# Linear attention and a Fourier gate on one core: a new order of work on all five engines, the negated filter spectrum read from PSUM, zero matmuls between PE's work

## The chip, the core and the metric

The kernel runs on one core of a Trainium2 chip. Inputs lie in the chip's memory as float32 and the output goes back there as float32. The metric is the time of one execution in device microseconds (us), as the median of several runs; lower is better. TensorE (PE) multiplies matrices into PSUM, VectorE (DVE), ScalarE (ACT) and GpSimd (POOL) work elementwise, and SyncE (SP) issues most transfers. Each engine works through its own list in order and waits where an operand is not there yet.

## The reference

```python
# r, k, v, w: (batch 4, heads 8, seq 768, head_dim 48); u: (8, 48)
for t in range(S):
    cur = np.einsum('bhd,bhe->bhde', u[None] * kt, vt)
    y[:, :, t] = np.einsum('bhd,bhde->bhe', rt, state + cur)
    state = wt[:, :, :, None] * state + np.einsum('bhd,bhe->bhde', kt, vt)
# x: y as (4, 768, 384)
proj = x @ w_proj                      # 384 x 1152
x1, x2, x3 = proj split in three
X2 = np.fft.rfft(x2, n=S, axis=1)
H = np.fft.rfft(filter_fft, n=S, axis=0)[None, :, :]
out = (x1 * np.fft.irfft(X2 * H, n=S, axis=1) * x3) @ w_out
```

The first half is a recurrence with a decay `w` and a bonus `u`, for 32 pairs of batch and head. The second half is a gate: three projections, a circular convolution by Fourier transforms over the sequence, two products and an output projection.

## The kernel before

The sequence is cut into 24 chunks of 128 steps, 6 to a batch. Chunks are loaded in groups: 0 and 1 alone, then pairs. A load (`lw`, `lk`, `lr`, `lv`) brings one chunk of w, k, r or v, 192 KB in pieces of 192 bytes, through SP's queue. Three buffers hold w and four each hold k with r, and v.

A group takes the logarithm of w (`ln`, ACT, L1250), a bf16 copy of v (`vb`), the product r k (`rk`), times u (`ru`), halves it by an add (`rh`), sums it over a head (`cc`, DVE, L1263) and multiplies v by the sums (`vc`, the bonus term, L1158). Any of `rk`, `ru`, `rh` stands on POOL or DVE, as the order says.

A chunk then goes through these steps: sums of the logarithms by triangular matmuls (`cs`, PE, L1278 to L1281), their exponential in PSUM (`ex`, ACT, L1284), the products with k and r (`kq`, DVE, L1287), the decay of the chunk (`ph`, ACT), eight transposes (`tr`, PE, L1299) and their copy (`qk`, DVE or ACT), the scores (`sc`, PE, L1311), the causal mask (`mt`, with `D` or `M` a product with a mask on DVE, L1327, with `A` or `N` a copy on ACT that POOL cuts afterwards, `mc`, L1332; `M`, `N` and `C` take both halves at once), the state (`ki`, `kv` on PE, `su` on DVE, L1362), the output of the chunk in PSUM (`yi` puts in the bonus term by two matmuls, `ys` the state's part, `y` the scores' part), its copy to `xn`, three transposes (`yt`) and their copy into `xT` (L1164 or L1162). Where `yi` is `-`, `xn` has the letter `V` and adds the bonus term on DVE (L1401).

Once a batch is whole, `second(b)` runs: the projections `p` and `q` (L1536) and `xw` (L1573), their copies `cp`, `cxw` and the product `cq`, folded sums and differences `sd`, the forward transform `f` with its copy `cf`, the products with the filter's spectrum `u0`, `u1`, `p`, the inverse transform `E` with its copy `cE` and two adds `aE`, the gate product `yE`, and the output `o` with its copy `co` and its store `so`. Batches overlap: one batch's second half runs between the chunks of the next. Projection weights come through POOL's queue (`wproj0` to `wproj2`, L1227, float32 to bf16 on the way).

The filter's spectrum is made once (`spectrum`, L1493): `filt` is one load of 1152 KB through SP's queue, `fsd0` and `fsd1` fold it on DVE (L1498), `h0` to `h2` transform it on PE into two PSUM banks each, `hc` scales it on ACT into `hh[:, 0]` (L1504), and `hg` on DVE copies the real part (L1510) and writes the negated imaginary part (L1514) into `hh[:, 1]`, from `hh[:, 0]`, which lies in SBUF. The tables of the inverse transform get their mirrored parts by four sign multiplications (`if`, L1482 to L1486).

What runs where and when is one list, `ORDER`, written out in the source: a line has a step's name, its engine's letter, the PSUM bank where it needs one, and in some lines another step's name. `Plan.run` (L1040) emits the steps in that order. The last name, where there is one, ties a step to an earlier DVE step: it waits until that one is done. `warm n b` emits `n` matmuls of zeros, 256 wide, into bank `b` (L1191). The list in before starts with 30 of them. Further on the list runs as

```
lk7 S
lk6 S
lr6 S
...
filt S
```

and has `if` on POOL between `mc9.0` and `rk6`, `wproj1` behind `mc3.1` and `wproj0` behind `mc4.0`.

Of the kernel before, what the change touches and what calls it, by code (L numbers as in the profile page):

```python
# [181 lines left out]
mc3.1 G
wproj1 G
ex4 A
cc2 D
kq4 D
ph4 A
su3 D
yt1 P 1
xT1 D  # L190
vc2 G su2
mc3.0 -
xT0 D
ex5 A
kq5 D
ph5 A
tr4 P 0
yi3 P 2
yi2 P 4
ys3 P  # L200
ys2 P
y3 P
y2 P
lr6 S
qk4 D
lr7 S
# [31 lines left out]
cxw0.0 D
lv7 S
mc4.0 G mt5.0  # L240
yi4 P 3
ys5 P
ys4 P
y4 P
mc5.0 -
xn4 A
y5 P
xn5 D
cs6 P 0
lv6 S  # L250
lw9 S
yt4 P 2
# [11 lines left out]
cxw0.4 A
lk8 S
lr9 S
lv8 S
tr6 P 5
# [11 lines left out]
wproj0 G  # L280
lv9 S
lw10 S
p0.2.1 P 4
p0.2.0 P 5
cf0.0 A
mt6.0 N
p0.0.1 P 0
rk4 D
sd0.1.0 D
cp0.2.0 D  # L290
f0.2 P 5
p0.0.0 P 2
# [1 line left out]
cp0.0.0 A
sc7 P 6
lr10 S
lr11 S
lw11 S
ru4 D
cp0.0.1 D  # L300
fsd0 D
mc6.0 C
ln5 A
lk11 S
fsd1 D
h1 P 0
mt7.0 M
h2 P 2
lv10 S
mc6.1 -  # L310
# [12 lines left out]
lv13 S
kv6 P 3
hg2 D
su6 D
mc7.1 -
yi6 - 2
hc0 A
hg0 D  # L330
cs8 P 0
yi7 P 4
# [1 line left out]
y6 P
ys7 P
ex8 A
y7 P
xn6 V
cs9 P 6
xn7 A  # L340
ki7 P 2
kv7 P
kq8 D
yt7 P 3
yt6 P 5
tr8 P 4
su7 D
lr12 S
lv11 S
# [52 lines left out]
ln6 A
q0.0.0 P 4
u00.0 D
cq0.0.1 D
q0.2.0 P 7
ki9 P 6
# [50 lines left out]
mc10.1 -
y10 P
xn10 A  # L460
mt11.1 -
kq12 D
su10 D
cs13 P 6
lk14 S
lk15 S
ex13 A
lw14 S
mc11.1 -
lr15 S  # L470
lw15 S
lk16 S
lv14 S
E0.0 P 3
# [152 lines left out]
mc14.1 -
y14 P
ln10 A
ex17 A  # L630
kq17 D
xw2.0 P 4
# [1 line left out]
mc15.0 -
xn14 A
mt16.0 A
ph17 A
yi15 P 2
ys15 P
y15 P  # L640
cxw2.0 A
xn15 A
cs18 P 6
# [45 lines left out]
ys16 P
q2.0.0 P 4  # L690
mc16.0 G
cq2.2.0 D
mt17.0 N
su18 D
y16 P
mt17.1 -
ln11 A
mc17.1 -
lv23 S
o0.0 P 2  # L700
rk11 G cc10
mc17.0 C
ru11 G
vc10 G rh10
xn16 V
sc18 P 0
lv22 S
cs20 P 6
co0.0 A
mt18.1 -  # L710
cq2.0.0 D
ex20 A
mt18.0 M
tr19 P 5
o0.1 P 2
# [1075 lines left out]
```

## Time and profile before

| what | value |
|---|---|
| runs | 166.23, 167.73 and 168.83 us; median 167.73 |
| profiled execution | 167.69 us, of it 165.9 in the span from the first to the last instruction |
| mean granted PE clock | 0.931 of full speed |
| busy, share of the span | PE 144.2 us (87%), DVE 140.3 (85%), ACT 117.7 (71%), POOL 99.3 (60%) |
| chain that ended last | PE 29%, DVE 22%, POOL 15%, DMA 12%, issue 11%, ACT 7% |
| memory | 22.41 MB read and 4.72 MB written, 164 GB/s over the span |

The page divides the span into 40 equal slices; a digit is the busy share in tenths. "Idle before" is the time an engine stood still just ahead of an instruction, with the one whose end released it behind an arrow. A matmul's own duration has its way through the array in it; what one costs in a row is the distance between starts. A line number such as L1158 can be that of a helper with many uses, so the tile's name beside it says which step it is.

### The profile page before, as it was taken

The page shows a single profiled execution, that of the slowest core. Times are in us where ns is not written, and L with a number is a line of the kernel's source. Part 1 is how long each engine was busy: PE and PEld are TensorE (multiplying, and loading weights), DVE is VectorE, ACT ScalarE, POOL GpSimd, SP SyncE. Part 2 cuts the span into 40 slices and gives each one's busy share as a digit, 9 for nine tenths or more (in the row PEclk, how much of TensorE's full clock was granted, in tenths as well). Part 3 has the DMA queues.
Part 4 walks back from the last instruction along what each step waited for, and adds up shares of the span by engine and source line. Part 5 has one row for each costly group of instructions (what it writes and reads, how often), then busy time and mean ns, then how long its engine had stood idle before and what let it go on. Part 6 is the DMA issues. An engine that isn't in the chain of part 4 may idle for free.

```text
span 165.9 us, 4290 instructions
## 1 busy us (share of the span) xinstructions
PE 144.2 (87%) x1665; PEld 94.9 (57%) x1665; DVE 140.3 (85%) x259; ACT 117.7 (71%) x192; POOL 99.3 (60%) x103
## 2 busy tenths in 40 slices
PE   7868877984984999649999999999989999999980
PEld 5538655652543667344666677667567666655530
DVE  6758999892799889375899999999999999999950
ACT  4997956674274686634998988878989866785460
POOL 7967796602227059985695799699269680330320
PEclk9965999998699599965999999999999999999997
DMA  5999999899999989999999999900250000200936
GB/s 107 212 212 215 207 199 203 161 287 194 211 212 175 203 166 205 184 217 214 201 192 217 191 211 184 175 11 0 96 194 0 4 0 4 95 2 19 356 133 254
DMA packets 104118, 26.23 MB, mean 158 GB/s; under 512 B 100129, under 2 KB 102690, under 8 KB 104098
## 3 DMA queue, kind: packets, MB, share of 16 engines
q1 hardware_dynamic: 102498, 24.78, 68.1%
q0 software_dynamic: 1600, 1.18, 5.0%
...
HBM read 22.41 MB, written 4.72 MB: 164 GB/s over the span
## 4 chain that ended last, share of the span: by engine, by line
PE 29%; DVE 22%; POOL 15%; DMA 12%; issue 11%; ACT 7%; SPq 1%; POOLq 0%; ACTq 0%; DVEq 0%
PE banks L1536 6%; POOL rk L1158 6%; DMA wproj<-in_moe_w_proj_dram 5%; PE banks L1438 5%; PE banks L1299 4%; DMA out_dram<-o 3%; PE banks L1692 3%; PE banks L1573 3%; POOL mt L1332 3%; DVE kq L1287 3%; PE banks L1628 2%; DVE hh L1514 2%; DMA w<-in_w_dram 2%; DMA kr<-in_k_dram 2%; POOL vc L1158 2%
## 5 line engine op out<-in xcount | busy, mean ns | idle before, releaser
L1536 PE MATMUL banks<-xT,wproj 128*128 128x384 bf16 x144 | 29.8, 344 | 2.7 <-DMA wproj<-in_moe_w_proj_dram 2.1
L1332 POOL TENSOR_SCALAR_AFFINE_SELECT mt<-mt 128x512 bf16<-128x512 bf16 (+1 forms) x17 | 15.9, 937 | 16.5 <-ACT mt L1162 11.8
L1158 POOL TENSOR_TENSOR vc<-vb,cc 128x768 bf16<-128x768 bf16 (+1 forms) x13 | 18.3, 1410 | 10.6 <-DVE cc L1263 7.6
L1287 DVE TENSOR_TENSOR kq<-banks,kr 128x768 bf16<-128x768 f32 x24 | 22.7, 950 | 2.2 <-ACT banks L1284 1.9
L1162 ACT ACTIVATE x<-banks 128x768 bf16<-128x768 f32 (+1 forms) x26 | 18.0, 700 | 6.1 <-PE banks L1573 4.0
L1158 POOL TENSOR_TENSOR rk<-kr 128x768 bf16<-128x768 f32 (+1 forms) x12 | 20.1, 1679 | 2.6 <-DMA kr<-in_r_dram 1.3
L1299 PE MATMUL banks<-ident,kq 128*128 128x128 bf16 x192 | 16.8, 243 | 5.1 <-DVE kq L1287 4.5
L1536 PEld LDWEIGHTS <-wproj 128*128 128x128 bf16 x144 | 13.5, 102 | 11.9 <-DMA wproj<-in_moe_w_proj_dram 2.5
L1284 ACT ACTIVATE banks<-banks 128x768 f32<-128x768 f32 x24 | 19.1, 804 | 0.5 <-PE banks L1281 0.2
L1299 PEld LDWEIGHTS <-kq 128*128 128x128 bf16 x192 | 13.6, 110 | 7.3 <-DVE kq L1287 6.7
L1327 DVE TENSOR_TENSOR mt<-banks,mask_excl 128x512 bf16<-128x512 f32 (+1 forms) x17 | 15.6, 934 | 2.4 <-PE banks L1311 2.0
L1162 ACT ACTIVATE qk<-banks 128x1024 bf16<-128x1024 bf16 x14 | 14.1, 1028 | 2.4 <-PE banks L1299 2.3
L1162 ACT ACTIVATE X<-banks 128x768 bf16<-128x768 f32 x12 | 9.7, 811 | 7.8 <-PE banks L1438 7.5
L1162 ACT ACTIVATE mt<-banks 128x512 bf16<-128x512 f32 (+1 forms) x17 | 12.6, 749 | 3.7 <-PE banks L1311 3.1
L1158 POOL TENSOR_TENSOR y<-y,g 128x768 bf16<-128x768 bf16 (+1 forms) x6 | 8.1, 1354 | 11.6 <-PE banks L1628 9.0
L1438 PE MATMUL banks<-sd,F 128*128 128x384 bf16 (+1 forms) x96 | 14.0, 336 | 0.3 <-DVE sd L1584 0.3
L1573 PE MATMUL banks<-wproj,xT 128*128 128x384 bf16 x72 | 14.0, 333 | 0.1
L1692 PE MATMUL banks<-wout,y 128*128 128x384 bf16 x72 | 13.2, 326 | 0.0
L1438 PEld LDWEIGHTS <-F 128*128 128x128 bf16 (+1 forms) x120 | 9.1, 106 | 7.0 <-issue 2.9
L1561 DVE TENSOR_TENSOR g<-banks,x 128x384 bf16<-128x384 f32 (+1 forms) x16 | 11.6, 747 | 0.2 <-PE banks L1536 0.2
L1162 ACT ACTIVATE o<-banks 128x768 f32<-128x768 f32 (+1 forms) x12 | 9.1, 782 | 3.6 <-PE banks L1692 1.9
L1158 DVE TENSOR_TENSOR U<-X,hh 128x2304 bf16<-128x2304 bf16 (+1 forms) x12 | 11.1, 950 | 0.0
(110 smaller groups left out, 331.0 us busy)
## 6 DMA issues: line engine op xcount, KB each, us to landing
w<-in_w_dram SPq DMA_DIRECT2D x24, 192.0 KB, 3.9
kr<-in_r_dram SPq DMA_DIRECT2D x24, 192.0 KB, 3.8
kr<-in_k_dram SPq DMA_DIRECT2D x24, 192.0 KB, 3.8
v<-in_v_dram SPq DMA_DIRECT2D x24, 192.0 KB, 4.2
...
U<-in_moe_filter_fft_dram SPq DMA_DIRECT2D x1, 1152.0 KB, 9.3
wproj<-in_moe_w_proj_dram POOLq DMA_DIRECT2D x3, 288.0 KB, 5.8
out_dram<-o SPq DMA_DIRECT2D x2, 192.0 KB, 2.6
```

Of the source, the lines that this page charges most:

```text
L1158: return eng(e).tensor_mul(o, a, b)
L1162: return nc.scalar.activation(out=o, in_=a, func=AF.Copy)
L1284: op(f"ex{i}", [ACT], lambda e, bk: nc.scalar.activation(out=two(bk, f"cs{i}")[:, :, 0:C], in_=two(bk, f"cs{i}")[:, :, 0:C], func=AF.Exp), ...
L1287: op(f"kq{i}", [DVE], lambda e, bk: nc.vector.tensor_mul(kq[f][:, :, :, 0:D], two(bk, f"cs{i}")[:, :, 0:C].rearrange("p a (h d) -> p a h d ...
L1299: nc.tensor.transpose(p[:, HP * m + j, :], kq[f][:, m, 2 * j:2 * j + 2, :], ident)
L1327: return copy(ACT, o, x) if e in (ACT, ACT2) else nc.vector.tensor_mul(o, x, _mid(mask_excl, z - HP * a))
L1332: return nc.gpsimd.affine_select(out=o, in_=o, pattern=[[0, z - HP * a], [1, L]], compare_op=ALU.is_gt, fill=0.0, base=0, channel_multipli ...
L1438: nc.tensor.matmul(p[rows], F[:, ti, c0 + rows.start:c0 + rows.stop], x[q][:, ti, :], start=(ti == 0), stop=(ti == NT - 1),)
L1536: nc.tensor.matmul(p, wproj[:, cb, col0:col0 + L], xT[bx][:, cb, sl], start=(cb == 0), stop=(cb == CB - 1),)
L1561: op("c" + n3, [DVE], lambda e, bk: nc.vector.tensor_mul(g[bx][:, fs, sl], view(bk, n3), x1[:, fs, sl]), r=[f"x1.{fb}.{hf}" for fb in fbs] ...
L1573: nc.tensor.matmul(view(bk)[:, z], xT[bx][:, cb, (c0 + z) * L:(c0 + z + 1) * L], wproj[:, cb, C:2 * C], start=(cb == 0), stop=(cb == CB - 1),)
L1692: nc.tensor.matmul(view(bk)[:, z], yt_[:, z, :], wout[:, cb, :], start=(cb == 0), stop=(cb == CB - 1),)
```

## The change

It has four parts, and touches nothing of what is computed.

1. `hg` reads the imaginary part from PSUM, where `h` left it, and scales it by -2/S in the same instruction (for the first block by a column `neg0`, whose first row is 0). The first row of the copied block is still set by a copy and a memset. `hg` now counts as a user of the PSUM banks of `h`.
2. `warm` stands at nine places: 28 at the start, 11 behind `um`, then 2, 5, 3, 3, 7, 2 and 6, between the first chunks and the filter's transform. In all 67 in place of 30.
3. `xn` has a new letter `X`: ACT copies to a float32 buffer `xf`, and a new POOL step `xa` adds the bonus term and writes `xn`. One chunk, 18, uses it; for the others `xa` is `-`.
4. The whole list stands in another order, with other engines for some 80 steps and other banks and ties. Among them: `if` goes from POOL to DVE, ahead of chunk 6; `wproj1` and `wproj0` stand one behind the other; `p0.2.0`, `p0.0.0`, `p0.2.1` and `xw0.4` stand ahead of `cs6`; `rk4` goes to POOL; six `qk` go from DVE to ACT and one the other way; seven `xT` go from DVE to ACT and three back; `yi6` and `yi13` are added, `yi10`, `yi14` and `yi18` dropped; nine `mc` are added on POOL and nine dropped; `yE0.1`, `yE0.2`, `yE1.1` and `yE3.2.0` go from POOL to DVE and `yE1.0` the other way. Loads start `lk1 lw2 lr0 lk0` in place of `lw0 lr0 lk0 lk1`; `lw22` and `lw23` go out near the end.

```diff
-ADD, DVE2, ACT2, POOL2, FOLD = "V", "M", "N", "C", "Q"
+ADD, DVE2, ACT2, POOL2, FOLD, WIDE = "V", "M", "N", "C", "Q", "X"
...
-warm 30 7
+warm 28 7
...
+um P 1
+warm 11 7
...
+wproj1 G su1
+wproj0 G mt3.0
...
+kq5 D
...
+if D
+xT2 D
+vb3 G kq4
...
+warm 7 6
+sc6 P 4
...
+sc7 P 2
...
+warm 6 6
+h1 P 6
+mt7.1 D
+mt7.0 D
+mc6.1 -
+h2 P 0
...
-if G
-rk6 G rh5
...
+xn18 X
+q2.0.1 P 0
...
+xa18 G kq22
...
+    xf = sb.tile([L, NX, C], FP32, name="xf")
...
+    neg0 = sb.tile([L, 1], FP32, name="neg0")
...
+        nc.vector.memset(neg0, -2.0 / S)
+        nc.vector.memset(neg0[0:1, :], 0.0)
...
-            o = xn[:, i % NX].rearrange("p (j a d) -> p a j d", a=2, d=D)
+            o = (xf if e == WIDE else xn)[:, i % NX].rearrange("p (j a d) -> p a j d", a=2, d=D)
...
-            return copy(e, o, yview(bk))
...
+            return copy(ACT if e == WIDE else e, o, yview(bk))
...
+        op(f"xa{i}", [POOL, NONE], lambda e, bk: nc.gpsimd.tensor_add(
+            xn[:, i % NX], xf[:, i % NX], vcq.rearrange("p h d -> p (h d)")),
+           r=[f"xn.{i % NX}", f"vc.{fg}"], w=[f"xn.{i % NX}"])
...
                 nc.vector.tensor_scalar(
-                    out=hh[:, 1, 0, n, :], in0=hh[:, 0, 1, n, :], scalar1=-1.0, scalar2=None, op0=ALU.mult)
+                    out=hh[:, 1, 0, n, :], in0=two(bk, f"h{n}")[:, 1, 0:C], scalar1=-2.0 / S if n else neg0,
+                    scalar2=None, op0=ALU.mult)
...
-            op(f"hg{n}", [DVE], gcopy(n), r=[f"Hc.{n}"], w=[f"H.{n}"])
+            op(f"hg{n}", [DVE], gcopy(n), r=[f"Hc.{n}"], w=[f"H.{n}"], uses=[f"h{n}"])
```

More of the change, by code (lines that the diff above doesn't have):

```diff
@@ L180 @@
-ki3 P 4
-kv3 P
[L182 to L187, printed above, removed]
-su3 D
[L189 to L206, printed above, removed]
+lr6 S
+xT0 D
+yi3 P 6
+ys3 P
+y3 P
+ex5 A
+yi2 P 2
+ys2 P
+filt S
+kq4 D
+xn3 A
+mc2.0 -
+y2 P
+xn2 A
+lw9 S
+ph4 A
+wproj1 G su1
+wproj0 G mt3.0
+lv6 S
+xa3 -
+rk3 G xT0
+xa1 -
+tr4 P 6
+yt1 P 0
+kq5 D
+ki3 P 3
+xa2 -
+yt3 P 2
+lw8 S
+qk4 A
+ph5 A
+xT1 A
+lv7 S
+lr9 S
+lk9 S
+yt2 P 7
+kv3 P
@@ L235 @@
-yi5 P 5
 mc5.1 -
-ln4 A
[L238 to L252, printed above, removed]
+ys4 P
+y5 P
+y4 P
+p0.2.0 P 1
+xn5 D
+xa5 -
+yt5 P 2
+cxw0.0 A
+xn4 A
+xa4 -
+ln4 A
+yt4 P 5
 xT4 D
-yt5 P 5
+p0.0.0 P 6
 xT5 D
-cs7 P 3
+cp0.2.0 D
+lv8 S
+p0.2.1 P 4
+xw0.4 P 2
+cp0.0.0 A
+cs6 P 6
+cp0.2.1 A
+cs7 P 4
+p0.0.1 P 0
+cxw0.4 A
+sd0.0.0 D
+f0.0 P 2
 ex6 A
-lw8 S
 ex7 A
 kq6 D
-xw0.4 P 6
 kq7 D
 ph6 A
[L264 to L268, printed above, removed]
@@ L269 @@
-qk6 D
-tr7 P 0
-ph7 A
-lr8 S
-qk7 A
-lk9 S
-sd0.0.0 D
-sc6 P 2
+ph7 A
+rk4 G
+tr6 P 7
+lw10 S
+lw11 S
+sd0.1.0 D
+cp0.0.1 A
+tr7 P 4
+qk7 A
+f0.2 P 0
+qk6 A
+cf0.0 A
+warm 7 6
+sc6 P 4
+ru4 D
 mt6.1 -
-f0.0 P 6
+fsd0 D
+fsd1 D
+warm 2 6
+sc7 P 2
 lk10 S
[L280 to L292, printed above, removed]
-cf0.2 A
[L294 to L310, printed above, removed]
+lk11 S
+cf0.2 A
 rh4 D
 cc4 D
-mt7.1 -
+vb4 G
+mt6.0 N
+warm 6 6
[4 more added lines that the diff above has]
+h2 P 0
+mc7.0 -
+ln5 A
+vc4 G cc4
+mc7.1 -
 hc1 A
 hg1 D
-mc7.0 -
-h0 P 6
+h0 P 4
+mc6.0 C cc4
+kv6 P 3
 hc2 A
-cp0.2.1 A
-vb4 G xT4
-vc4 G fsd0
-lw13 S
[L323 to L332, printed above, removed]
-wproj2 G
[L334 to L349, printed above, removed]
@@ L350 @@
-ex9 A
-lr14 S
-xT6 D
+hg2 D
+lr11 S
+cs8 P 6
+hc0 A
+lk15 S
+ex8 A
+su6 D
+yi7 P 0
+ys7 P
+y7 P
+hg0 D
+xn7 A
+xa7 -
+lv11 S
+lw12 S
+lv10 S
+lk12 S
+lw13 S
+yi6 P 2
+y6 P
+cs9 P 4
+xn6 A
+yt7 P 1
+ex9 A
+xa6 -
+ki7 P 0
+kq8 D
+yt6 P 3
+xT7 D
+lr12 S
+kv7 P
+ph8 A
+wproj2 G
+xT6 D
+lk13 S
+tr8 P 1
+rk5 G hg0
+qk8 A
+xw1.0 P 6
 kq9 D
-lw12 S
-rk5 G
 ru5 D
@@ L397 @@
+mt9.1 A
+mc9.1 G
+mc9.0 G su7
+yi8 P 2
+q0.2.1 P 7
+u10.0 D
+cq0.0.1 D
+ln6 A
+lk14 S
+lr14 S
+ys9 P
+ys8 P
+y8 P
+cq0.2.1 D
+q0.0.0 P 0
+u00.0 D
 xn8 A
-yt8 P 6
-u10.0 D
-cq0.2.1 D
+xa8 -
+yt8 P 3
 xT8 A
[L402 to L407, printed above, removed]
-y9 P
+y9 P
+cs11 P 6
+xn9 A
+q0.2.0 P 2
 cq0.0.0 D
-xn9 A
-cs11 P 0
+ex11 A
+ki9 P 3
 kv9 P
-ex11 A
-yt9 P 3
+xa9 -
+yt9 P 0
+xT9 A
 cs10 P 4
 cq0.2.0 D
-xT9 A
+p1.2.0 P 2
+rk6 G cq0.2.1
 ex10 A
+kq11 D
+ph11 A
+ru6 D
 su9 D
-kq11 D
@@ L458 @@
[L458 to L461, printed above, removed]
-kq12 D
[L463 to L474, printed above, removed]
+lw16 S
+q1.0.0 P 0
+qk11 D
+sc10 P 4
+lr17 S
+vb6 G kq10
+vc6 G kq10
+mt10.1 A
+mc10.1 G cc6
+cq1.0.0 D
+sc11 P 6
+mt11.1 A
+mc11.1 G
+mt10.0 D
+yi10 - 4
+q1.2.0 P 3
+ki10 P 2
+lr16 S
+lk16 S
+lv16 S
+cs12 P 0
+mt11.0 A
+cq1.2.0 D
+mc11.0 G qk11
+mc10.0 -
+ys10 P
+y10 P
+xn10 V
+cs13 P 6
+rk7 G
+ru7 G
+rh7 G
+kv10 P
+ex12 A
+ex13 A
+kq12 D
+xa10 -
 yt10 P 5
-tr12 P 2
@@ L627 @@
[L627 to L632, printed above, removed]
-mt16.1 D
[L634 to L643, printed above, removed]
+xn13 A
+xa13 -
+cs17 P 0
+tr16 P 6
+ex17 A
+lw21 S
+yt13 P 4
+xT13 A
+yt12 P 5
+qk16 D
+ys14 P
+xT12 A
+y14 P
+ki16 P 7
+kv16 P
+mc15.1 -
+lk21 S
+lr20 S
+lk20 S
+ln10 A
+sc16 P 4
+mt16.0 A
+xn14 V
+kq17 D
+lv21 S
+xa14 -
+yt14 P 6
+lk22 S
+lv20 S
+xw2.0 P 2
+mc15.0 -
+ph17 A
+lr23 S
+yi15 P 0
+ys15 P
+rk9 G mt15.0
+xT14 A
+ru9 D
+rh9 G qk16
+cxw2.0 A
@@ L686 @@
-yi16 - 6
-sc17 P 2
-cc10 D
[L689 to L715, printed above, removed]
+cc9 D
+q2.2.0 P 2
+cs19 P 4
+qk17 A
+ex19 A
+p2.0.0 P 0
+lw23 S
+ph18 A
+vc9 G
+tr18 P 3
+kq19 D
+cp2.0.0 A
+xw2.2 P 6
+vb10 A
+qk18 D
+p2.2.0 P 1
+ph19 A
+sc17 P 4
+cxw2.2 A
+kv18 P 3
+q2.0.0 P 6
+yE0.2 D
+mc16.0 G
```

1072 lines of the change are left out of this document (525 added, 547 removed).

## The prediction

> **What bounds the kernel now.** I read the page's slices first, then a table of four stretches, then the timeline of each engine at the stretches' borders. The borders are the first k-by-decay products (`kq`, L1287) of chunks 6, 8 and 12, since nothing of a chunk runs on VectorE before its own.
>
> ```profile
> span 165.9 us, 4290 instructions
> PE   7868877984984999649999999999989999999980
> DVE  6758999892799889375899999999999999999950
> PEclk9965999998699599965999999999999999999997
> DMA  5999999899999989999999999900250000200936
> 33.30:54.60 21.30, 15.49 (x138) 8.76 (x137) 16.98 (x24) 11.02 (x17) 6.25 (x5) 0.91 1.06 215
> 54.60:80.20 25.60, 21.86 (x247) 14.46 (x246) 17.91 (x26) 16.27 (x28) 17.20 (x14) 0.81 1.01 199
> 80.20:159.20 79.00, 78.17 (x924) 51.36 (x922) 78.18 (x139) 63.30 (x107) 49.83 (x40) 1.00 0.47 110
> ```
>
> The columns of the last three rows are length, then busy time of PE, PEld, DVE, ACT and POOL, the granted clock, DMA share and GB/s. From 80.2 us on DVE and PE are both busy 78.2 of 79 us: that stretch costs what its work costs. Before it DVE stands 4.3 us idle in the second stretch and 7.7 us in the third, and the clock falls. The loads keep the DMA full to about 107 us, so nothing can come before its data. Time is to be had in the two middle stretches.
>
> ```profile
> 33.29 1.88 DVE L1287 TENSOR_TENSOR kq<-banks,kr 128x768 bf16<-128x768 f32 x2
> 43.91 2.62 DVE L1498 TENSOR_TENSOR P<-U 128x1152 bf16<-128x1152 f32 x2
> 48.77 1.53 DVE L1514 TENSOR_SCALAR hh<-hh 128x384 bf16<-128x384 bf16 x1
> 50.39 2.51 DVE L1514 TENSOR_SCALAR hh<-hh 128x384 bf16<-128x384 bf16 x1
> 53.96 0.26 DVE L1514 TENSOR_SCALAR hh<-hh 128x384 bf16<-128x384 bf16 x1
> 54.60 0.95 DVE L1287 TENSOR_TENSOR kq<-banks,kr 128x768 bf16<-128x768 f32 x1
> 48.66 1.52 POOL L1158 TENSOR_TENSOR vc<-vb,cc 128x768 bf16<-128x768 bf16 x1 [5.91 <-DVE cc L1263]
> 50.96 1.81 POOL L1158 TENSOR_TENSOR rk<-kr 128x768 bf16<-128x768 f32 x1
> L1510 DVE COPY hh<-hh 128x384 bf16<-128x384 bf16 x3 | 0.8, 250 | 0.1
> ```
>
> The same negation takes 0.26 us alone, 1.53 us where POOL's `vc` runs (to 50.18) and 2.51 us where `rk` runs (to 52.77): each time it ends just after POOL's product. The filter's spectrum thus holds DVE 4.3 us where 0.8 would do, ahead of chunk 8.
>
> ```profile
> 64.73 1.25 POOL L1482 TENSOR_SCALAR mi<-mi,sgn 128x384 bf16<-128x384 bf16 x1
> 65.97 2.45 POOL L1484 TENSOR_SCALAR mx<-mi,sgn 128x384 bf16<-128x384 bf16 x2
> 68.40 1.16 POOL L1486 TENSOR_SCALAR mi<-mi 128x384 bf16<-128x384 bf16 x1
> 69.53 1.79 POOL L1158 TENSOR_TENSOR rk<-kr 128x768 bf16<-128x768 f32 x1
> 71.36 0.56 DVE L1158 TENSOR_TENSOR rk<-rk,u_b 128x768 bf16<-128x768 bf16 x1 [3.68 <-POOL rk L1158]
> 72.84 1.89 PE L1299 MATMUL banks<-ident,kq 128*128 128x128 bf16 x16 [3.61 <-DVE kq L1287]
> 72.00:77.00 5.00, 4.16 (x30) 2.79 (x30) 3.27 (x4) 2.63 (x4) 4.28 (x3) 0.50 1.08 211
> 77.33 0.69 DVE L1327 TENSOR_TENSOR mt<-banks,mask_excl 128x512 bf16<-128x512 f32 x1 [1.80 <-PE banks L1311]
> 80.25 0.96 DVE L1287 TENSOR_TENSOR kq<-banks,kr 128x768 bf16<-128x768 f32 x1 [0.65 <-ACT banks L1284]
> ```
>
> The four sign flips (`if`) hold POOL 4.86 us, `rk6` starts late, DVE's `ru6` waits 3.68 us for it, `kq10` stands behind `ru6`, PE pauses 3.61 us, and the next 5 us run at clock 0.50, where DVE waits another 1.80 us.
>
> **The change part by part.** Prices of moved work:
>
> ```profile
> L1164 DVE CAST xn<-banks 128x384 bf16<-128x384 f32 x2 | 1.1, 552 | 0.1
> L1164 DVE COPY xT<-banks 128x384 bf16<-128x384 bf16 x13 | 4.4, 351 | 1.0 <-PE banks L1409 0.6 <-ACT banks L1284 0.2
> L1164 DVE COPY qk<-banks 128x1024 bf16<-128x1024 bf16 x10 | 6.8, 684 | 1.3 <-PE banks L1299 1.2
> L1162 ACT ACTIVATE qk<-banks 128x1024 bf16<-128x1024 bf16 x14 | 14.1, 1028 | 2.4 <-PE banks L1299 2.3
> L1193 PE MATMUL banks<-wt 128*128 128x256 bf16 x30 | 6.1, 394 | 1.1 <-DVE scl L1208 1.1
> 135.89 0.98 PE banks L1692 x6
> ```
>
> *Second stretch (chunk 6 to chunk 8).* The negation now reads PSUM. Its nearest row is the cast of 384 f32 from PSUM at 0.55 us, which stayed there whatever POOL did: three cost 1.7 for 4.3 us. Also gone from DVE here: `qk6` 0.68, `rk4` and `cp0.0.1` (768 wide, like the `kq` row) 0.95 each, `xn6` 0.55, and two small ones that run earlier. About 7 of its 17 us leave, so DVE no longer sets this stretch. What is late next is the filter:
>
> ```profile
> 30.78 0.88 SPq L1495 DMA_DIRECT2D U<-in_moe_filter_fft_dram  x1
> U<-in_moe_filter_fft_dram SPq DMA_DIRECT2D x1, 1152.0 KB, 9.3
> 46.58 3.19 PE L1438 MATMUL banks<-P,F 128*64 128x384 bf16 x23 [0.46 <-DVE P L1498]
> 50.69 0.82 ACT L1284 ACTIVATE banks<-banks 128x768 f32<-128x768 f32 x1
> 43.27 1.22 SPq L1244 DMA_DIRECT2D kr<-in_r_dram  x1
> kr<-in_r_dram SPq DMA_DIRECT2D x24, 192.0 KB, 3.8
> 31.08 8.62 DMA wproj<-in_moe_w_proj_dram
> wproj<-in_moe_w_proj_dram POOLq DMA_DIRECT2D x3, 288.0 KB, 5.8
> ```
>
> It lands at 30.78 + 9.3 = 40.1 (its place in SP's queue, number 31, is kept). Then the two sums 2.62, the transforms 3.2, ACT's last scaling 1.0 and `hg0` 1.3 (copies 0.25 each, one negation): 48.2. The other arm, `cs8` and its exponential (0.9 + 0.8 after the transforms), is ready at 47.6, and r of chunk 8 lands at 43.27 + 3.8 = 47.1. So `kq8` can start at 48.2 at best; before it was 54.6. PE does 2.9 us more ahead of `cs6` (`p0.2.0`, `p0.0.0`, `p0.2.1`, `xw0.4`: 18 matmuls of 0.163), which it no longer does later, and that still leaves `h1` waiting for the filter at 42.7. It needs `wproj0` at about 32; POOL now issues that right behind `wproj1`, near 24, and the median issue lands in 5.8. `cs8` shares banks 6 and 7 with `h1`, `yi7` 0 with `h2`, `cs9` 4 with `h0`, so PE, with all behind it, now waits for `hg1`, `hg2`, `hg0`; DVE is free for them. I take 49.9, the best case plus one POOL product (1.5) in front of a copy: a gain of 4.7, between 6.4 and 1.0 (53.6, if every copy and flip waits for POOL).
>
> *Third stretch (chunk 8 to chunk 12).* The flips go to DVE, in front of chunk 6's work: four at 0.26 alone, at most 2.51 each; the first stretch has the room for 1 us of it (its DVE work is otherwise level). POOL goes from `mc9.0` straight to `rk6`, tied to `cq0.2.1`, which DVE has done by then. That ends the 3.68 us wait. Without the pause most of the 1.80 us behind it goes too; I take 1.0. DVE gains 0.9 of work (`xT7` 0.35, `xn10` 0.55). Net 3.8, between 0 and 4.6.
>
> *Fourth stretch.* Twenty-odd copies, masks and adds change engine. DVE loses on balance five `xT` (0.35 each), one `qk` (0.68), two `rh` and three `sd` (384 wide, bf16, 0.35 to 0.9 each) and gains one `ru`, `cE0.1`, three gate products, one `dE` (0.35 to 0.6 each) and about 1 us of masks: at most 1.2 gained, an estimate from these widths. ACT gets some 2.5 more (the `xT` and the `qk`, 1.03) beside 63.3 of 79, which can cost up to 2. PE's work is level (over the whole, two `yi` in, three out; `xn18` with one POOL add stands in for one pair). I take 0.5.
>
> *Zero matmuls.* The first 28 stand for the old 30. Eleven follow `um`, where PE waited for the first decay sums anyway. Of the other 26, at 256/384 of 0.163 = 0.11 us each, 2.8 us in all at full clock, I count half as uncovered: 1.4, between 0 and 5.6 (all, at half clock). Loads, stores and the order of stages behind chunk 12 are otherwise nearly as before; `lw22` and `lw23` go out 6 and 4 places later, about 105 us, still ahead of `ln12`.
>
> Sum on the profiled span: 165.9 - 4.7 - 3.8 - 0.5 + 1.4 = 158.3; with the 1.8 us that this run took beyond its span (167.69, at the median of 167.73) 160.1 us.
>
> Page and trace, in sentences of their own. The Trainium skill (SBUF — State Buffer, section "SBUF: two separate sides") says that VectorE in a two-port mode and GpSimd hold the shared port pair exclusively for a whole instruction. The negations above agree (ends 50.30 and 52.90 behind 50.18 and 52.77). By that rule the moved flips and the remaining copies can each still wait for a whole POOL product, which speaks against this change. The skill (TensorE: Matmul & The Clock Gate, section "HAM oscillation") sets the harmful idle gap at about 3.4 us; the 3.61 us pause and clock 0.50 agree; by it the zero matmuls, at most 0.8 us together, matter only where they split such a gap, and the sum would keep the 1.0 of the third stretch.
>
> **The rivals.** *The projection weights come late (no change to slightly faster).* In before the chain of waits spends 8.6 us on the landing of one `wproj`, and two issues now follow each other. If `wproj0` came at 39 instead of 32, `cs6` and all behind it on PE would slip 7 us, of which the wait for the filter absorbs about 1.7: 160.1 + 5.3 = 165.4. For it: the full DMA. Against: the median of 5.8.
>
> *DVE waits for POOL at the flips and copies (slower).* Four flips and three copies are short two-port operations. At x us each instead of 0.25 they cost 7 (x - 0.25) over 158.6, the sum without its one POOL product: with the mean of the three negations, 1.43, 8.3 us and 166.9; at 2.51, 15.8 us and 174.4. It passes before + 2% (171.1) at about x = 2, longer than one `rk` product of 1.8. For it: the rows above. Against: the three copies took 0.25 each in before, and `vb3` and `rk5` are tied behind neighbours.
>
> *The change does not do what it says:* PSUM reads that still wait for POOL would give back 2.6 us: 162.7, inside the range.
>
> **How the numbers follow.** The sum, between 155.5 (all upper gains, no cost) and 163.5: 0.64. Late weights or a stage that takes the gain back, 163.5 to 169: 0.24. DVE held by POOL, above that: 0.12. The likeliest is 160.1. The range of 155.5 to 168 leaves out about 0.18. Measurements here tell about 2% (3.4 us) from no change: faster 0.65, same 0.23, slower 0.12.
>
> **What would show it.** Right: negations of about 0.55 us, `kq8` near 50, no 3.6 us PE pause before `kq10`, `kq12` near 72, and then 85 us to the end as before. Wrong: flips of over 1 us on DVE, a PE wait for `wproj` above 2 us, `h1` later than 45, or a last stretch longer than 86 us.

## The result, and the profile after

The changed kernel takes 158.40 us in the median of 4 runs (156.00 to 159.40). Beside it the kernel before took 167.34 us (4 runs, 166.23 to 168.83). The ratio is 0.9385 with a 95% interval of 0.9243 to 0.9528: faster, by 9 us between the medians. The ratio leaves out runs more than 1.5% above the fastest of their kernel, so for the changed kernel it rests on the runs of 156.00 and 157.43 us, and the profiled execution is not one of them. The forecast was 160.1. The profiled execution of the changed kernel took 159.36 us, 157.7 of it in the span; the numbers below are of that one execution, against the 165.9 us of before.

The first lines are from the page of the changed kernel (its head, the busy times, and the slices in tenths); they answer to the slices shown of before.

```profile
span 157.7 us, 4363 instructions
PE 143.0 (91%) x1700; PEld 95.2 (60%) x1700; DVE 135.1 (86%) x259; ACT 123.0 (78%) x203; POOL 96.4 (61%) x102
PE   7678885899999599999999999999999999999990
DVE  6849989804797987999999989999999999799960
PEclk9999999569999959999999999999999999999999
DMA  5999999999999999899998999982400002200746
```

The pause of PE before chunk 10 and the half clock behind it are gone: from the 16th slice on PE shows a 9 up to the last one, and the clock is full. What stays low lies between 27 and 39 us (clock 5 and 6 in the 8th and 9th slice, DVE 0 and 4 in the 9th and 10th) and behind 51 us (PE 5 in the 14th, clock 5 in the 15th). PE's busy time fell by 1.2 us only (144.2 to 143.0); the rest of the 8.2 us was waiting.

The table of stretches, with the same borders as before (`kq` of chunks 6, 8 and 12; the columns are length, busy time of PE, PEld, DVE, ACT and POOL, granted clock, DMA share, GB/s):

```profile
0.00:41.00 41.00, 33.09 (x395) 22.77 (x396) 27.98 (x74) 29.98 (x46) 25.97 (x42) 0.92 1.03 208
41.00:54.60 13.60, 11.49 (x128) 7.13 (x127) 12.52 (x21) 10.30 (x17) 5.89 (x5) 1.00 1.08 197
54.60:74.60 20.00, 19.91 (x254) 13.40 (x252) 18.36 (x29) 16.18 (x30) 12.58 (x11) 0.91 1.01 200
74.60:152.60 78.00, 77.70 (x922) 51.56 (x923) 75.66 (x139) 65.53 (x114) 51.94 (x45) 1.00 0.53 126
```

| stretch | before | after | gained | forecast |
|---|---|---|---|---|
| start to `kq8` | 54.6 | 54.6 | 0.0 | 4.7 |
| `kq8` to `kq12` | 25.6 | 20.0 | 5.6 | 3.8 |
| `kq12` to the end of the span | 85.7 | 83.1 | 2.6 | 0.5 |
| zero matmuls | | | | -1.4 |
| sum | 165.9 | 157.7 | 8.2 | 7.6 |

The sum was met and its terms were not. The first row reads differently in other executions: three of the experiments below (`f1_copies_dve`, `f2_rh_dve`, `f3_zeros_late`) have the very list of the changed kernel up to chunk 8, and reached `kq8` at 52.3, 52.8 and 51.4 us. So the changed kernel gains between 0 and 3.2 us there, and the profiled execution is the worst of these four; the other three gain 1.8 to 3.2. The next row is steadier: from `kq8` to `kq12` those three took 18.6 to 19.9 us, and before's list took 24.6 to 25.6 in its three profiled executions (before, `e8_before_neg_psum`, `g1_before_rh_pool`).

The timeline of DVE, POOL, SP and PE around the two parts that were to gain time ahead of chunk 8 (start, busy time, engine, line, operation; idle time before it in brackets):

```profile
24.15 1.82 POOL L1192 TENSOR_TENSOR rk<-kr 128x768 bf16<-128x768 f32 x1
25.91 0.83 POOL L1198 CAST vb<-v 128x768 bf16<-128x768 f32 x1
24.87 2.00 DVE L1522 TENSOR_SCALAR mi<-mi,sgn 128x384 bf16<-128x384 bf16 x1
26.78 0.54 DVE L1524 TENSOR_SCALAR mx<-mi,sgn 128x384 bf16<-128x384 bf16 x2
27.24 0.25 DVE L1526 TENSOR_SCALAR mi<-mi 128x384 bf16<-128x384 bf16 x1
27.68 0.34 DVE L1398 TENSOR_TENSOR S<-banks,phi 128x192 bf16<-128x192 f32 x1
28.08 0.34 PE L1394 MATMUL banks<-S,ident 128*128 128x192 bf16 x1 [1.90 <-DVE S L1398]
30.91 3.95 PE L1614 MATMUL banks<-wproj,xT 128*128 128x384 bf16 x12
31.31 0.77 SPq L1535 DMA_DIRECT2D U<-in_moe_filter_fft_dram  x1
35.90 0.56 DVE L1198 CAST xn<-banks 128x384 bf16<-128x384 f32 x1 [4.20 <-PE banks L1425]
43.92 1.35 DVE L1538 TENSOR_TENSOR P<-U 128x1152 bf16<-128x1152 f32 x1
47.46 3.22 PE L1478 MATMUL banks<-P,F 128*64 128x384 bf16 x24
50.58 2.18 DVE L1550 COPY hh<-hh 128x384 bf16<-128x384 bf16 x1
50.82 1.81 POOL L1192 TENSOR_TENSOR rk<-kr 128x768 bf16<-128x768 f32 x1
52.68 0.55 DVE L1554 TENSOR_SCALAR hh<-banks 128x384 bf16<-128x384 f32 x1
```

The row at 47.46 is the filter's transform, `h1` first. Two things are to be seen. The flips, now on DVE, run beside POOL's `rk` and `vb`: the first one takes 2.00 us, where the last takes 0.25. The chunk's state `S` behind them comes late, and PE pauses 1.90 us for it. And the negation from PSUM costs the 0.55 us that were forecast, but the copy in front of it, which still reads SBUF, now waits for POOL's `rk5` (to 52.63): 2.18 us in place of 0.25. The wait moved one instruction ahead. The list ties `rk5` to `hg0`, which should keep the two apart; but `rk5` starts at 50.82, before `hg0` has begun. The cause is in the source: a tie waits for the instruction that the step's function returns, and the function `gcopy`, which issues `hg`, returns none, so the tie is empty.

### The profile page after: what moved, and what is told of

The parts are those of the page before. It is cut to its first block, busy times and chain, and to the rows that moved or that the text cites. A ratio compares the mean times of both kernels' runs of the same rounds, so it can differ in the third digit from the quotient of the medians.

```text
span 157.7 us, 4363 instructions
## 1 busy us (share of the span) xinstructions
PE 143.0 (91%) x1700; PEld 95.2 (60%) x1700; DVE 135.1 (86%) x259; ACT 123.0 (78%) x203; POOL 96.4 (61%) x102
## 4 chain that ended last, share of the span: by engine, by line
PE 68%; ACT 7%; DVE 6%; SPq 6%; issue 4%; POOL 4%; DMA 3%; DVEq 0%; POOLq 0%; ACTq 0%
PE banks L1577 15%; PE banks L1614 9%; PE banks L1478 7%; PE banks L1669 6%; PE banks L1733 6%; SPq L1280 5%; PE banks L1335 5%; PE banks L1347 3%; PE banks L1425 3%; PE banks L1449 3%; DMA kr<-in_k_dram 3%; PE banks L1388 2%; DVE hh L1550 2%; PE banks L1417 2%; PE banks L1315 2%
## 5 line engine op out<-in xcount | busy, mean ns | idle before, releaser
L1192 POOL TENSOR_TENSOR rk<-kr 128x768 bf16<-128x768 f32 (+1 forms) x13 | 24.4, 1879 | 7.6 <-DMA kr<-in_r_dram 5.1
L1577 PE MATMUL banks<-xT,wproj 128*128 128x384 bf16 x144 | 27.8, 326 | 0.0
L1196 ACT ACTIVATE qk<-banks 128x1024 bf16<-128x1024 bf16 x19 | 19.3, 1028 | 1.4 <-PE banks L1335 1.4
L1363 DVE TENSOR_TENSOR mt<-banks,mask_excl 128x512 bf16<-128x512 f32 (+1 forms) x22 | 17.7, 829 | 1.5 <-ACT x L1196 0.9
L1614 PE MATMUL banks<-wproj,xT 128*128 128x384 bf16 x72 | 16.1, 371 | 0.0
L1368 POOL TENSOR_SCALAR_AFFINE_SELECT mt<-mt 128x512 bf16<-128x512 bf16 (+1 forms) x17 | 12.8, 766 | 5.0 <-ACT mt L1196 3.8
L1335 PE MATMUL banks<-ident,kq 128*128 128x128 bf16 x192 | 14.8, 223 | 0.9 <-DVE kq L1323 0.6
L1478 PE MATMUL banks<-sd,F 128*128 128x384 bf16 (+1 forms) x96 | 13.3, 328 | 0.4 <-ACT x L1196 0.3
L1335 PEld LDWEIGHTS <-kq 128*128 128x128 bf16 x192 | 11.8, 99 | 2.9 <-DVE kq L1323 1.1
L1196 ACT ACTIVATE mt<-banks 128x512 bf16<-128x512 f32 (+1 forms) x17 | 11.1, 682 | 2.8 <-DVE S L1398 2.8
L1198 POOL CAST vb<-v 128x768 bf16<-128x768 f32 (+1 forms) x6 | 5.9, 976 | 10.9 <-DMA v<-in_v_dram 5.6
L1602 DVE TENSOR_TENSOR g<-banks,x 128x768 bf16<-128x768 f32 (+1 forms) x16 | 11.8, 753 | 0.2 <-PE banks L1577 0.2
L1227 PE MATMUL banks<-wt 128*128 128x256 bf16 x67 | 10.9, 314 | 1.1 <-DVE scl L1242 1.1
```

The source lines that it names most:

```text
L1192: return eng(e).tensor_mul(o, a, b)
L1196: return nc.scalar.activation(out=o, in_=a, func=AF.Copy)
L1335: nc.tensor.transpose(p[:, HP * m + j, :], kq[f][:, m, 2 * j:2 * j + 2, :], ident)
L1363: return copy(ACT, o, x) if e in (ACT, ACT2) else nc.vector.tensor_mul(o, x, _mid(mask_excl, z - HP * a))
L1368: return nc.gpsimd.affine_select(out=o, in_=o, pattern=[[0, z - HP * a], [1, L]], compare_op=ALU.is_gt, fill=0.0, base=0, channel_multipli ...
L1478: nc.tensor.matmul(p[rows], F[:, ti, c0 + rows.start:c0 + rows.stop], x[q][:, ti, :], start=(ti == 0), stop=(ti == NT - 1),)
```

## The experiments

All times of `kq` and stretches are of the profiled execution of each. Executions of nearly equal lists differ by 1 to 3 us in when they reach chunk 8 (above), so a change ahead of chunk 8 is read from the stretch that holds it, and the total only with its interval.

**The flips back on POOL.** The kernel after, with one step put where before has it:

```diff
 kv3 P
-if D
...
 mc9.0 G su7
+if G
...
 rk6 G cq0.2.1
```

> The changed kernel with one step put back: the four sign flips run on POOL between mc9.0 and rk6 again, as in the kernel before. In the changed kernel kq6, kq8 and kq12 start at 41.0, 54.6 and 74.6 us. Theory (the third stretch was bound by rk6 standing behind the flips): kq8 to kq12 goes from 20.0 back to 24 us or more, with a PE pause of over 3 us before tr10 and half clock behind it; in return kq6 comes some 3 us earlier, since the flips no longer hold DVE 2.6 us ahead of su3; total 157 to 161 us. Rival (the new order shortens that stretch whatever POOL does): kq8 to kq12 stays at 20 to 21 us and the total falls to about 155.

Measured: 161.80 us (161.23 to 166.01), ratio to before 0.9656 (0.961 to 0.9702), whose interval lies wholly above that of after. `kq8` to `kq12` takes 24.6 us for 20.0. Its POOL timeline, and then two rows of its waits in that stretch (engine, line, releaser, sum, times, longest):

```profile
61.25 1.25 POOL L1522 TENSOR_SCALAR mi<-mi,sgn 128x384 bf16<-128x384 bf16 x1
62.49 2.87 POOL L1524 TENSOR_SCALAR mx<-mi,sgn 128x384 bf16<-128x384 bf16 x2
65.34 1.16 POOL L1526 TENSOR_SCALAR mi<-mi 128x384 bf16<-128x384 bf16 x1
66.48 1.80 POOL L1192 TENSOR_TENSOR rk<-kr 128x768 bf16<-128x768 f32 x1
```

```profile
DVE rk L1192 <- POOL rk L1192: 3.1, 1, 3.1
PE banks L1335 <- DVE kq L1323: 2.9, 1, 2.9
```

The chain of before is back, link by link: 5.25 us of flips on POOL, `rk6` behind them, 3.1 us of DVE waiting, 2.9 us of PE waiting. Of the 4.6 us lost here, `kq8` had given 2.8 back (51.8 for 54.6), though executions of the unchanged list show the same earlier `kq8`, so that part isn't certain.

**The flips moved in the kernel before, and nothing else.**

```diff
 kq5 D
+if D
...
-if G
 rk6 G rh5
```

> The kernel before with one step alone changed: the flips on DVE behind kq5, everything else as before. Theory (with the flips off POOL, rk6 follows mc9.0 at once): kq8 to kq12 falls from 25.6 to 20 to 22 us with no PE pause ahead of tr10; the flips cost up to 3 us on DVE ahead of su3; total 163 to 165.5 us. Rival (the third stretch got shorter through the rest of the new order): kq8 to kq12 stays above 24 us, total 167 to 170.

Measured: 161.11 us (160.25 to 162.93), ratio 0.9602 (0.953 to 0.9674). The stretch from `kq8` to `kq12`, and that from there to the end:

```profile
54.90:73.40 18.50, 18.35 (x246) 12.23 (x246) 17.52 (x26) 16.08 (x28) 12.32 (x10) 1.00 1.02 202
73.40:158.50 85.10, 79.93 (x934) 52.18 (x932) 77.67 (x140) 65.51 (x109) 51.72 (x40) 0.99 0.55 134
```

25.6 us became 18.5 (24.6 to 25.6 in the executions of before's list), with PE busy throughout and the clock at 1.00. This one line of the list brings 6.4 us between the medians (167.47 for before beside it, less 161.11), and by the ratios 4.0 of the 6.2% of the whole change: about two thirds. The rest of the new list does not improve on this stretch: after takes 20.0 us there, and 18.6 in an execution without half clock (`f3_zeros_late`).

**The negation from SBUF again**, in the kernel after:

```diff
-                    out=hh[:, 1, 0, n, :], in0=two(bk, f"h{n}")[:, 1, 0:C], scalar1=-2.0 / S if n else neg0,
-                    scalar2=None, op0=ALU.mult)
+                    out=hh[:, 1, 0, n, :], in0=hh[:, 0, 1, n, :], scalar1=-1.0, scalar2=None, op0=ALU.mult)
...
-            op(f"hg{n}", [DVE], gcopy(n), r=[f"Hc.{n}"], w=[f"H.{n}"], uses=[f"h{n}"])
+            op(f"hg{n}", [DVE], gcopy(n), r=[f"Hc.{n}"], w=[f"H.{n}"])
```

> The changed kernel with the negation of the spectrum reading SBUF again, as before. The prediction's step: the negations then take up to 2.5 us each where POOL works, kq8 comes 2 us or more later and the total rises by 2 to 2.6 us. Rival (the wait for POOL belongs to whichever short two-port instruction comes first; in this order it is the copy ahead of the negation, 2.18 us in hg2, so the negation finds POOL done): negations 0.26 us but for one, kq8 within 0.7 us of 54.6, total within 1 us.

Measured: 158.81 us (157.73 to 159.54), ratio 0.9484 (0.9429 to 0.9539), which overlaps the interval of after; by the total alone a loss of the forecast size isn't excluded. `kq6` to `kq8`, where the step lies, takes 13.6 us, as in after. Its timeline:

```profile
49.31 1.15 DVE L1554 TENSOR_SCALAR hh<-hh 128x384 bf16<-128x384 bf16 x1
50.38 0.24 DVE L1550 COPY hh<-hh 128x384 bf16<-128x384 bf16 x1
50.55 2.50 DVE L1554 TENSOR_SCALAR hh<-hh 128x384 bf16<-128x384 bf16 x1
51.12 1.81 POOL L1192 TENSOR_TENSOR rk<-kr 128x768 bf16<-128x768 f32 x1
```

Now the negations wait and the copies take 0.25 us. Whichever of the SBUF operations meets an operation of POOL pays for it.

**The negation from PSUM alone, in the kernel before.** Here the negation of the second block reads a bank that a later step of chunk 6 (`kv6`) has already overwritten, since before's list gives that bank away earlier: that part of the filter's spectrum is changed, and the instruction's size is not.

```diff
+    neg0 = sb.tile([L, 1], FP32, name="neg0")
...
-                    out=hh[:, 1, 0, n, :], in0=hh[:, 0, 1, n, :], scalar1=-1.0, scalar2=None, op0=ALU.mult)
+                    out=hh[:, 1, 0, n, :], in0=two(bk, f"h{n}")[:, 1, 0:C], scalar1=-2.0 / S if n else neg0,
+                    scalar2=None, op0=ALU.mult)
...
-            op(f"hg{n}", [DVE], gcopy(n), r=[f"Hc.{n}"], w=[f"H.{n}"])
+            op(f"hg{n}", [DVE], gcopy(n), r=[f"Hc.{n}"], w=[f"H.{n}"], uses=[f"h{n}"])
```

> The kernel before with the negation from PSUM alone. The prediction's term: three negations of 0.55 us instead of 4.3 us in all, kq8 2 us or more earlier, total 1.5 to 2.6 us less. Rival (the wait passes to the copy ahead of it, as in the changed kernel): the copies take over 1.5 us together, kq8 within 1 us of 54.6, total within 1 us of before.

Measured: 167.37 us (10 runs, 165.51 to 169.04), ratio 0.9985 (0.9941 to 1.0029): no gain. Its timeline:

```profile
49.11 1.52 POOL L1159 TENSOR_TENSOR vc<-vb,cc 128x768 bf16<-128x768 bf16 x1 [5.95 <-DVE cc L1266]
49.22 0.55 DVE L1517 TENSOR_SCALAR hh<-banks 128x384 bf16<-128x384 f32 x1
51.40 1.95 DVE L1513 COPY hh<-hh 128x384 bf16<-128x384 bf16 x1
51.41 1.82 POOL L1159 TENSOR_TENSOR rk<-kr 128x768 bf16<-128x768 f32 x1
```

The first negation runs in 0.55 us in the middle of POOL's `vc`: a read of PSUM does not wait, as forecast. The copy of the last block meets `rk5` and takes 1.95 us. `kq8` comes at 54.8, as in before (54.6).

**The tie made real**, in the kernel after:

```diff
-                nc.vector.tensor_scalar(
+                return nc.vector.tensor_scalar(
```

> The changed kernel with the step hg returning its last instruction, so that the tie of rk5 to hg0 in the list takes effect (in the changed kernel rk5 starts at 50.82 us, ahead of hg0 at 53.41, so the tie does nothing). Theory (hg2's copy waits 1.9 us for rk5): the copy takes 0.25 us, kq8 starts near 52.7 instead of 54.6, total 1 to 2 us less. Rival (rk5 then comes later and ru5, vc5 with it, or kq8 is not what the end hangs on): copy 0.25 us, but total within 0.7 us.

Measured: 156.36 us (154.82 to 157.02), ratio 0.9329 (0.9261 to 0.9398).

```profile
51.50 0.30 DVE L1550 COPY hh<-hh 128x384 bf16<-128x384 bf16 x1
51.72 0.54 DVE L1554 TENSOR_SCALAR hh<-banks 128x384 bf16<-128x384 f32 x1
53.79 1.81 POOL L1192 TENSOR_TENSOR rk<-kr 128x768 bf16<-128x768 f32 x1 [2.05 <-DVE hh L1554]
```

POOL now waits 2.05 us for `hg0`, and the copy that took 2.18 us takes 0.30. `kq6` to `kq8` falls to 12.2 us, where the eight executions of the changed kernel and its variants without this tie show 13.3 to 13.6. The total's interval overlaps that of after, so the gain rests on the stretch: 1.1 to 1.4 us.

**The flips later on DVE**, where DVE waits anyway, in the kernel after:

```diff
 kv3 P
-if D
...
 mt5.0 D
+if D
```

> The changed kernel with the four flips still on DVE but later, behind mt5.0, where DVE stood idle 4.2 us (31.7 to 35.9), instead of ahead of su3. Theory (ahead of su3 the first flip waits 1.7 us for POOL, su3 and with it PE's ki4 come late, and PE drops to half clock over the first projections): ki4 near 25.5 instead of 28.1, no half clock between 26 and 38 us, kq6 by 38 instead of 41.0, kq8 by 52, total 1.5 to 3 us less. Rival 1 (kq6 waits for the loads of chunks 6 and 7, rk4 for r at 34.6): kq6 moves by less than 1 us, total within 1 us. Rival 2: the flips find POOL at work in the new place too and nothing is gained.

Measured: 157.33 us (154.96 to 158.27). The first flip fell to 0.45 us and those behind it took 0.25 to 1.14. `kq6` came at 39.0 and `kq8` at 52.3, inside what lists with the flips in their old place show (38.1 to 41.4, 51.4 to 54.6): not told apart.

**Both together.** The edits of the last two runs in one kernel.

> Both repairs on the changed kernel: flips behind mt5.0, and the tie of rk5 to hg0 made real (alone that gave kq8 to kq12 18.6 instead of 20.0 us and 156.4 us). If they act in different places they add: 153 to 155 us. Rival: the second stretch then hangs on something else (filter, loads) and the sum is no better than the better of the two, 155.5 to 156.5.

Measured: 155.82 us (155.61 to 157.46), ratio 0.9325 (0.9263 to 0.9387); the copies take 0.26 us each, `kq6` to `kq8` 11.8 us. It is the fastest version tried, some 2.6 us below the changed kernel's median and 0.6% by the ratios, though the intervals overlap and it is not to be told from the one with the tie alone.

**No zero matmuls but the first 28**, in the kernel after (39 matmuls taken out):

```diff
 um P 1
-warm 11 7
...
-warm 7 6
 sc6 P 4
...
-warm 2 6
...
-warm 6 6
 h1 P 6
```

> The changed kernel without the eight later groups of zero matmuls (39 of 67); the first 28 stay. Theory (they fill time in which PE waits anyway, and are too few to hold the clock): total within 1 us of the changed kernel, same mean clock within 0.01. Rival 1 (half of the 26 lie on the path, as the prediction had it): 1.4 us faster. Rival 2 (they keep the clock up): one or two more stretches of 3.4 us at half clock, mean clock down by 0.01 to 0.02, total 2 us or more slower.

Measured: 157.59 us (156.33 to 159.62), ratio 0.9456 (0.9376 to 0.9537), against 0.9385 of after with overlapping intervals: not told apart. `kq8` at 52.0 is inside the spread of after's list. The mean clock of its runs was 0.954 to 0.974, that of after's 0.967 to 0.989; the ranges overlap, so whether the zero matmuls help to keep the clock up stays open.

That the total doesn't show them does not make them free. First the transform `h1` of this kernel, then, of `f2_rh_dve` (it has the zero matmuls), the eleven behind `um` and the first decay sum, then that sum in after:

```profile
43.98 3.22 PE L1470 MATMUL banks<-P,F 128*64 128x384 bf16 x24
```

```profile
8.71 2.53 PE L1227 MATMUL banks<-wt 128*128 128x256 bf16 x11
11.03 0.53 PE L1314 MATMUL banks<-lg,mask_neg 128*128 128x384 bf16 x1
```

```profile
9.71 0.32 PE L1314 MATMUL banks<-lg,mask_neg 128*128 128x384 bf16 x1 [0.85 <-ACT lg L1286]
```

Without the zero matmuls `h1` comes 5.6 us behind `kq6` (38.35), with them 6.4 us (41.05 to 47.46 in after): 0.8 us of the fifteen in between lie on PE's way. `kq6` to `kq8` takes 13.6 us all the same: ACT works without a pause there, so its scaling `hc1` starts 7.4 us behind `kq6` instead of 7.6, and the copies behind it still meet POOL (0.87 and 2.20 us). And the eleven behind `um`, which cost nothing in after, where PE waits for ACT, fell into half clock in `f2_rh_dve`: the first decay sum came 1.3 us later than in after.

**What sets the fourth stretch: more copies on DVE.** Eight copies go from ACT to DVE, in the kernel after:

```diff
-xT10 A
+xT10 D
...
-qk15 A
+qk15 D
```

(and the same for `xT11`, `xT13`, `xT14`, `xT16`, `xT20` and `qk20`).

> The changed kernel with eight copies behind chunk 10 put back from ACT to DVE at their places in the list (xT10, xT11, xT13, xT14, xT16, xT20, qk15, qk20): 6 x 0.35 + 2 x 0.68 = 3.5 us more on DVE, 5.0 us less on ACT. The stretch from kq12 to the end of the span took 83.1 us in the changed kernel and 85.7 in the one before. Theory 1 (DVE's work sets that stretch): it grows by 2.5 to 3.5 us. Theory 2 (PE sets it, DVE has the 2.3 us that it stands idle there): it grows by less than 1 us.

Measured: 160.95 us (160.46 to 162.89), ratio 0.959 (0.9478 to 0.9702). From `kq12` to the end:

```profile
72.00:159.30 87.30, 79.69 (x932) 51.96 (x926) 78.86 (x148) 63.76 (x107) 52.01 (x45) 0.99 0.56 136
```

87.3 us for 83.1, with eight copies worth 3.5 us added (six at 0.35, two at 0.68): 4.2 us more, above the 2.5 to 3.5 of theory 1. DVE has no slack there; what makes up the last 0.7 us was not followed up. The growth is clear of noise: six other kernels here (`e1` to `e6`) have after's list behind `kq12`, and each took 83.0 to 83.3 us for it.

**The same by more work on PE.** Twenty zero matmuls go in front of the scores of ten chunks from 14 to 23:

```diff
+warm 2 5
...
+warm 2 2
```

(and eight more such lines).

> The changed kernel with two zero matmuls of 256 columns in front of the scores of chunks 14 to 23, in the bank that the scores then write: 20 x 0.11 = 2.2 us more work on PE in the last stretch. If PE sets it (theory 2), kq12 to the end goes from 83.1 to about 85.3; if DVE does (theory 1), it stays within 0.7 us; if the two take turns, about half, 84.2.

Measured: 157.97 us (156.97 to 161.41), ratio 0.9428 (0.9319 to 0.9538). A stretch ahead of `kq6`, then `kq12` to the end:

```profile
27.00:38.10 11.10, 9.90 (x121) 6.53 (x122) 6.48 (x16) 7.07 (x11) 4.39 (x4) 1.00 1.08 240
70.00:155.20 85.20, 80.91 (x952) 53.15 (x946) 77.25 (x140) 67.07 (x115) 52.03 (x45) 0.99 0.58 141
```

85.2 for 83.1: 2.1 of the 2.2 us of added work (20 at 0.11) appear. So PE has no slack either, and neither theory alone holds. That the two engines alternate, each waiting for the other with no room left, is read from these two runs and not shown by itself: the zero matmuls stand ahead of scores that DVE's masks wait for, and no others were tried. The first row is of use for the second stretch. After, and then `f1_copies_dve`, have the same list there:

```profile
27.00:41.00 14.00, 12.89 (x121) 7.80 (x122) 6.46 (x16) 6.80 (x11) 4.33 (x3) 0.76 1.07 239
```

```profile
27.00:39.00 12.00, 11.56 (x121) 7.28 (x122) 5.94 (x14) 6.86 (x11) 5.15 (x4) 0.86 1.06 237
```

The same 121 matmuls up to `kq6` fill 14.0 us at clock 0.76, 12.0 at 0.86 and 11.1 at 1.00 (in `f2_rh_dve` too, from 28.40 to 39.50).

**Two halving adds on DVE again**, in the kernel after:

```diff
-rh9 G qk16
+rh9 D
...
-rh11 G
+rh11 D
```

> The changed kernel with rh9 and rh11 on DVE, as before, where rh11 stood 1.7 us beside a POOL product. Theory 1 (DVE sets the last stretch): kq12 to the end goes from 83.1 to 84.5 or more. Theory 2 (PE sets it): 83.1 to 83.6.

Measured: 161.43 us (159.36 to 162.40), ratio 0.9594 (0.9482 to 0.9706); `kq12` to the end 87.0 us, 3.9 more, though the two adds took 0.36 us each. Its timeline says where the rest is:

```profile
95.04 0.80 POOL L1267 DMA_DIRECT2D wout<-in_moe_w_out_dram  x1 [1.56 <-DVE S L1398]
95.25 3.65 DVE L1192 TENSOR_TENSOR U<-X,hh 128x2304 bf16<-128x2304 bf16 x1
95.86 1.82 POOL L1192 TENSOR_TENSOR rk<-kr 128x768 bf16<-128x768 f32 x1
```

Without `rh9`, POOL's issue of the `wout` load and its `rk10` lie across DVE's wide product `u11.0`, which ends 1.22 us behind `rk10`: 3.65 us, where after shows 1.43. Why `rk10`, 0.61 us younger, came first is not shown; the issue lay across the start of `u11.0`. A second meeting near 114 us, of `sd2.0.0` and `ru11` with the two masks that POOL runs behind `rk12`, costs 0.9 more. With the adds themselves (0.7) that is 3.8 of the 3.9.

**Two halving adds on POOL, in the kernel before**, the other way round:

```diff
-rh9 D
+rh9 G
...
-rh11 D
+rh11 G
```

> The kernel before with one thing of the change: the two halving adds rh9 and rh11 go from DVE to POOL, nothing else moves. In before they took 0.87 and 1.71 us on DVE (2.58 together), the second because POOL's rk12 ran until 117.23. After has them on POOL and its stretch from kq12 to the end is 2.6 us shorter (83.1 for 85.7). Theory 1, these two adds are what the fourth stretch gained, by DVE's relief: kq12 to the end falls to 83.1 to 84.0, the total to 165.3 to 166. Theory 2, the gain there is that of the whole new arrangement: the stretch stays at 85.1 or above, and the total within 0.6 us of before. Theory 3, the adds on POOL (0.9 to 1.4 us each) hold cc9 and cc11 up: the stretch grows beyond 86.

Before's own rows first, then those of this kernel:

```profile
105.24 0.87 DVE L1260 TENSOR_TENSOR rk<-rk 128x384 bf16<-128x384 bf16 x1
115.73 1.71 DVE L1260 TENSOR_TENSOR rk<-rk 128x384 bf16<-128x384 bf16 x1
```

```profile
114.56 1.82 POOL L1158 TENSOR_TENSOR rk<-kr 128x768 bf16<-128x768 f32 x1
114.85 2.75 DVE L1158 TENSOR_TENSOR U<-X,hh 128x2304 bf16<-128x2304 bf16 x1
```

Measured: 167.70 us (166.53 to 168.71) beside 167.04 for before, ratio 1.0131 (0.9988 to 1.0274): no gain, and a loss isn't excluded. `kq12` to the end takes 85.3 us for 85.7, inside the 85.1 to 85.8 that `e7_before_flips_dve` and `e8_before_neg_psum` show with before's list there. The 1.71 us of `rh11` beside `rk12` are gone, and `u01.0`, the next DVE operation that reads SBUF twice, stands there and takes 2.75 us. The relief is handed on, as with the filter's copy. Theory 2 of this run holds.

## Why the forecast came out right, step by step

*The flips leave POOL (third stretch): right in mechanism, too small.* The waits went as forecast: no pause of PE and no 3.68 us wait of `ru6`. The term was sized at 3.8 with an upper end of 4.6; it measured 5.6 in after and 7.1 in the kernel before with this step alone. What was too small is the 1.0 us put on "the 1.80 us behind it": without the pause the half clock went as well. By e7's row PE's idle time there fell from 3.7 to 0.2 us, and its busy time, which the half clock had stretched, from 21.9 to 18.4: 3.6 and 3.5 us, and the forecast priced only the first in full.

*The second stretch: this step failed.* It was sized at 4.7 us and measured 0 in the profiled execution, 1.8 to 3.2 in the three others of the same list. (The forecast's own sum, 48.2 and one POOL product of 1.5, makes 49.7 and not 49.9.) "What is late next is the filter" is wrong: it was issued at 31.31 and landed 6.9 us later, at about 38.2, and the sum that needs it starts at 43.92, behind `kq6` in DVE's list. What is late is PE. Its projection matmuls ahead of `cs6`, which the forecast counted as absorbed by the wait for the filter, stand on the path: PE runs without a pause of note from 28.08 until `cs6`, and DVE waits 4.20 us for it. `h1`, forecast at 42.7, starts at 44.5 at full clock (`f3_zeros_late`) and at 47.5 in after. The whole error lies ahead of `h1`: from there to `kq8` the forecast had 7.2 us, and after took 7.1. So 1.8 us of it appear at full clock too, and 2.9 us more go with the half clock from 27.8 on, which the forecast did not have. This is read from the timelines; no run put the projection matmuls back, so their share is not measured by itself. Two of the forecast's four signs of being wrong came true here, a flip of over 1 us on DVE and `h1` later than 45.

*The negation from PSUM: right in price, wrong in effect.* 0.55 us, and it doesn't wait, as `e8_before_neg_psum` shows; but the forecast counted the whole of the old wait as saved (2.6 us), and the copy ahead of it took it over. Taking this part away from after did not move the stretch, and adding it alone to before did not move the time.

*DVE waits for POOL at flips and copies: this rival named a true mechanism.* The first flip took 2.00 and the copies 2.18 and 0.67 us: 4.1 us above 0.25 each, where the rival had 8.3 and decided only near 12. It didn't decide, since the other flips and copies met no product. Its argument that a wait can hardly be longer than one `rk` product did not hold: the first flip waited through two POOL operations, `rk` and then `vb` (to 26.74), and took 2.00 us. The page's rule in the forecast (the Trainium skill, SBUF — State Buffer, section "SBUF: two separate sides") agrees with all these rows: the waiting operation ends behind POOL's, by its own length or less.

*The fourth stretch: too small.* Forecast 0.5, measured 2.6. The DVE work there fell from 78.18 to 75.66 us, twice the 1.2 that the forecast allowed at most. One part was mis-sized from the widths: the two `rh` were taken at 0.35 to 0.9 us, and in before they took 0.87 and 1.71. Yet moving these two alone gains nothing (`g1_before_rh_pool`). The order of POOL's list matters too: `u11.0` takes 1.43 us in after, where `rk10` starts 0.97 us behind it and is the one that waits (2.13 us for 1.82), and took 3.65 as soon as POOL's order shifted (`f2_rh_dve`). That the gain comes from the arrangement as a whole, with DVE and PE both without slack, fits the four runs but is not shown; which of its some 80 moves carry it was not tried one by one.

*Zero matmuls: forecast to cost 1.4, not seen in the total.* The forecast counted 26 of them behind the eleven; there are 28, which moves its term by 0.1 us. Of these, 0.8 us lie ahead of `h1`, and ACT's queue hid most of that. The eleven behind `um`, which were to be free, cost 1.3 us in an execution where half clock met them.

*The projection weights* were not waited for: in after no engine stood idle until one of them landed, and `xw` starts at 30.91 straight behind PE's other work, so this rival is out.

So the total was right by luck, since errors of both signs cancelled: 4.7 us too much in one term, 1.8 and 2.1 too little in two others, and 1.4 charged for the zero matmuls, which are already in the measured stretches.
